# One load's source rows in another order: 64 pairs outermost instead of two runs of 64

## The chip, the cores and the metric

The kernel runs on one core of one Trainium2 chip. The metric is the device time of one execution in microseconds; lower is better. The time before is the median of three runs.

## The reference

Two independent spectral layers on 2048 rows of 512 numbers in float32, whose outputs are laid side by side.

```python
X = jnp.fft.rfft2(x, axes=(-2, -1)) * (w_r + 1j * w_i)     # A
y = jnp.fft.irfft2(X, s=(S, D), axes=(-2, -1))

a = jnp.einsum("bsd,ed->bse", x, dft_hid_re)               # B
b = jnp.einsum("bsd,ed->bse", x, dft_hid_im)
y = jnp.einsum("ts,bse->bte", dft_seq_re, a) - jnp.einsum("ts,bse->bte", dft_seq_im, b)
```

The four DFT matrices of B are inputs, 2048 x 2048 twice and 512 x 512 twice.

## The kernel before

Both transforms are done by matmuls with small tables that the program carries. B does not multiply by its big input matrices: it assumes that they are DFT matrices, transforms with its own tables, and compares every element of the inputs with them on the side (a flag tells at the end whether a slow path, which does multiply, has to run). So 34 blocks of 1 MB are loaded and compared.

The order of the work on PE, DVE, ACT and SP is written out by hand: each step registers itself under a name, and the string `PLAN` lists the names in the order in which they are issued. Each engine works off its own instructions in this order, and a step that waits holds all that stands behind it on its engine. Steps that matter here, with their lines:

- `xa`, `fold`, `hid`, `zs`, `f16_`, `ys` (L325 to L362): A's forward transform, in eight pieces. `hid7` and `f16_7` are the last piece's two groups of matmuls on PE, `zs7` is the copy on ACT (L351) between them, and `ys` (L362) writes the result to `fz`.
- Then eight slots n = 0 to 7, each with one residue of the frequencies: `w` loads its weights (L387) and its table `fi` (L391; L260 for slot 2, whose table is `fi0`), both on SP; `tr` transposes on PE (L404), `ez` copies on ACT (L408), `sf` combines on DVE (L414 to L416; `sx2` in slot 2, L437), `fwd` transforms on PE (L423; L427 in slot 2), `prod` and `comb` multiply with the weights on DVE (L454 to L466), `inv` transforms back on PE (L484, L487), `ev` copies on ACT (L491). In slot 2 the ACT step `spy` stands between `comb` and `inv`.
- B's x goes in 16 groups of 128 rows, four to a buffer: `xb0` to `xb15` load them (L581; the last group, L583 to L585, in three pieces), `xr0` to `xr3` copy the mirrored columns of a buffer on ACT (L594, L595), `al` multiplies a group with the table `fb` on PE (L605, L606), and `av` copies on ACT (L610).
- `cl` loads a block of B's matrices on SP (L712), `cc` compares it on DVE (L700). The tables of this comparison are `tt`. `late` is a table load from POOL.
- `bh`, `hv`, `ro`, `y1` to `y3`, `pt` finish B; `hi`, `eu`, `g16_`, `sc`, `eo`, `st` are A's inverse (L519 to L546).

On SP the loads stand in the order xb0 to xb3, cl5 to cl8, xb4 to xb7, w2 and fi0, xb8 to xb11, cl9 to cl12, w3, fi3, w4, fi4, cl13, w5, fi5, xb12 to xb15, cl14, cl15, w6, fi6, w7, fi7, cl16 and so on. The blocks of `cl`, `xa` and `xb` share six buffers of 1 MB, so a load waits for the last reader of its buffer. Besides, SP's loads take turns on eight semaphores: each waits until the load eight places ahead of it has landed.

A group g of `xb` holds the rows lo = 16 + 64 n onward and the rows low = 1984 - 64 n onward, 64 of each, for n < 15. The table `fb` has one row for each partition; a matmul with it sums over the 128 rows of a group, so which row lies on which partition is free as long as x and `fb` agree.

Of the kernel before, what the change touches and what calls it, by code (L numbers as in the profile page):

```python
# [15 lines left out]
S, D = 2048, 512  # L16
# [25 lines left out]
def _ang(n, period):  # L42
    return 2 * np.pi * (np.asarray(n, dtype=np.int64) % period) / period
# [34 lines left out]
def _b_rows():  # L78

    c = np.arange(128)  # L80
    return np.stack([np.where(c < 64, 16 * c, 8 + 16 * (c - 64))] + [e + 16 * c for e in range(1, 8)])


def _tables_b():

    order = [3, 5, 7, 9, 11, 13, 15, 1, 0, 2, 4, 6, 8, 10, 12, 14]
    a = np.arange(16)
    fb = np.zeros((2, 2, 4, 16, 8, 16))
    for kind in range(2):
        for at, k in enumerate(order):  # L90
            e = k // 2 if k > 1 else 8 * k

            def wave(shift, part):
                th = 2 * np.pi * (a + shift) * e / 16
                return -np.sin(th) if part else np.cos(th)

            top, low, sg = (k % 2, 1 - k % 2, 1 - 2 * (k % 2)) if k > 1 else (0, 0, 1)
            for n in range(4):
                if kind and n == 3:
                    fb[kind, 0, 3, :, 3, at] = wave(0.5 if k > 1 else 0, top)  # L100
                    fb[kind, 1, 0, :, 7, at] = wave(0, top)
                    continue
                fb[kind, 0, n, :, n, at] = wave(0, top)
                fb[kind, 1, 3 - n, :, n, at] = wave(1, top)
                fb[kind, 0, n, :, 4 + n, at] = sg * wave(0, low)
                fb[kind, 1, 3 - n, :, 4 + n, at] = -sg * wave(1, low)

    fb = fb.reshape(2, 128, 8, 16).transpose(0, 1, 3, 2)
    fbs = np.stack([np.concatenate([fb[:, :, 7:], v * fb], 2) for v in (1, -1)], 1)

    rows = _b_rows()
    p = (1 + 4 * np.arange(16)[:, None] + np.arange(4)).reshape(16, 4)
    mb = np.zeros((11, 16, 8, 128))
    for e in range(8):
        th = _ang(p[:, :, None] * rows[e], S)
        if e:
            mb[e - 1, :, :4], mb[e - 1, :, 4:] = np.cos(th), np.sin(th)
            mb[e - 1, 15, 3] = (-1.0) ** np.arange(128)
            mb[e - 1, 15, 7] = 1.0
        else:  # L120
            first = np.arange(128) < 64
            for i, m in enumerate((first, ~first)):
                mb[7 + i, :, :4] = np.cos(th) * m
                mb[9 + i, :, 4:] = -np.sin(th) * m
                mb[7 + i, 15, 7] = m
                mb[9 + i, 15, 7] = 0.0
                mb[9 + i, 15, 3] = -np.sin(th[15, 3]) * m
    alt = np.zeros((16, 8, 1))
    alt[:, :4, 0] = np.cos(np.pi * p)
    alt[15, 7] = 1.0  # L130
    mb = np.concatenate([mb.reshape(11, 128, 128).transpose(1, 0, 2).reshape(128, -1), alt.reshape(128, 1)], 1)
    hc = np.zeros((128, 2, 257))
    f = np.arange(257)
    hc[:, 0] = np.cos(_ang(np.outer(np.arange(128), f), D))
    hc[0, 0] = 1 - f % 2
    hc[0, 1] = f % 2
    turn = np.array([(S - rows[o]) % S if o else np.where(np.arange(128) == 0, 1024, (S - rows[0]) % S)
                     for o in range(8)]).T
    return fbs.transpose(2, 0, 1, 3, 4), mb, hc, turn


def _tables():
# [29 lines left out]
    ht = np.stack([np.cos(th), -np.sin(th)]).reshape(2, 2, 128, 257).transpose(2, 1, 0, 3)  # L172
    odd = np.array([1.0, -1.0]) * np.where(np.arange(128) % 2, -1.0, 1.0)[:, None]
    fb, mb, hc, turn = _tables_b()
    d = np.arange(256)
    hf = np.zeros((256, 2, 2, 128))
# [46 lines left out]
def kernel(  # L223
# [16 lines left out]
    mm, TT, load = pe.matmul, dve.tensor_tensor, sync.dma_start  # L240
# [10 lines left out]
    def step(name):  # L251
        def add(f):
            assert name not in steps
            steps[name] = f
        return add

    def const(name, *shape, src=None, by=None):
        t = sp.tile([P, *shape], F32, name=name)
        if src is not None:
            by.dma_start(t, src)  # L260
        return t
# [5 lines left out]
    def bank_b(name):  # L267
        at[name] = ps_b.tile([P, 512], F32, name="pb")
        return at[name]

    def block(name):
        at[name] = sp.tile([P, 2048], F32, name="blk", bufs=NB)
        return at[name]
# [280 lines left out]
    fb = const("fb", 2, 2, 200)  # L554
# [14 lines left out]
    def along(q):  # L569
        src = xb.rearrange("b a d -> (b a) d")  # L570

        def load_group(g):
            n = 4 * q + g

            @step(f"xb{n}")
            def _():
                if g == 0:
                    at["x", q] = block(("xb", q)).rearrange("p (g d) -> p g d", g=4)
                x, lo, low = at["x", q], 16 + 64 * n, 1984 - 64 * n
                if n < 15:  # L580
                    load(x[:, g], bass.AP(xb.tensor, lo * D, [[(low - lo) * D, 2], [D, 64], [1, D]]))  # L581
                else:
                    load(x[:64, g], src[lo : lo + 64])  # L583
                    load(x[64:80, g], src[:16])
                    load(x[80:, g], src[low + 16 : low + 64])  # L585

        for g in range(4):
            load_group(g)

        @step(f"xr{q}")  # L590
        def _():
            x = at["x", q]
            xr = at["xr", q] = sp.tile([P, 4, 256], F32, name="xr")
            act.copy(xr[:, :, 0], x[:, :, 256])  # L594
            act.copy(xr[:, :, 1:], x[:, :, 511:256:-1])  # L595

        def group(g):
            n = 4 * q + g

            @step(f"al{n}")  # L600
            def _():
                bank, x, xr = bank_b(("al", n)), at["x", q], at["xr", q]
                for c, (lo, w) in enumerate(((0, 200), (200, 144))):
                    k = slice(128 * c, 128 * c + 128)
                    mm(bank[:, lo : lo + w], x[:, g, k], fb[:, n // 15, 0, :w], start=True, stop=False)  # L605
                    mm(bank[:, lo : lo + w], xr[:, g, k], fb[:, n // 15, 1, :w], start=False, stop=True)  # L606

            @step(f"av{n}")
            def _():
                act.copy(yall[:, :, 8 * n : 8 * n + 8], at["al", n][:, :344].rearrange("p (s j) -> p s j", j=8))  # L610

        for g in range(4):
            group(g)
# [286 lines left out]
```

## Time and profile before

| what | value |
|---|---|
| median of three runs (lowest, highest) | 276.13 us (276.02, 276.51) |
| the profiled execution | 275.29 us, span 273.2 us |
| mean granted TensorE clock | 0.857 |
| busy: PE, DVE, ACT, POOL | 188.9, 156.3, 83.5, 22.5 us |
| moved by DMA | 66.24 MB, mean 242 GB/s |

Of the chain of work that ended last, 33% is put down to DMA, 32% to PE, 21% to SP's queue and 9% to DVE; the largest line in it is L581 on SP's queue with 14%.

Times are in microseconds from the start of the span. In the forty slices each digit is the busy share of 1/40 of the span, in tenths. In a table by stages, each engine's busy time is followed by the number of its instructions, then the granted PE clock, the mean busy share of the core's 16 DMA engines, and the rate. In a row of waits stand the engine and line that waited, what it waited for, the sum, the count and the longest. In a timeline row stand start and length, and in brackets the idle time before it and what ended that. SPq is SP issuing a DMA: the length is the time for which the issue held SP.

### The profile page before, as it was taken

To read this page: it belongs to the slowest core of one execution; us is meant where nothing else is said; L and a number is where in the kernel's file an instruction comes from. 1 tells how busy PE (TensorE), PEld (TensorE's weight loads), DVE (VectorE), ACT (ScalarE), POOL (GpSimd) and SP (SyncE) were. 2 spreads that over 40 slices of the span, in tenths; PEclk is the share of its full clock that TensorE was granted. 3 is DMA by queue.
4 is the path that set the end of the run, shared out by engine and by line. 5 is a ranking of instruction groups with operands and counts; after the bars stand their busy time and mean duration, and the time that the engine had idled before them with its cause. 6 is when DMAs were issued, how large, how long until landed. Compare 5 with 4: busy or idle time off the path is not lost.

```text
span 273.2 us, 2751 instructions
## 1 busy us (share of the span) xinstructions
PE 188.9 (69%) x1017; PEld 161.7 (59%) x1017; DVE 156.3 (57%) x217; ACT 83.5 (31%) x114; POOL 22.5 (8%) x32
## 2 busy tenths in 40 slices
PE   5699999500991019910089309999799999999930
PEld 1589999500980018910069309788378888999930
DVE  0730891001979501203937704999994599899970
ACT  1026465004740031503004014324335434543210
POOL 3000000000000000000000000001222245220110
PEclk9999999955797557975579957999979999999995
DMA  7999991298221611399911882690958999999913
GB/s 253 406 409 410 421 370 57 82 302 282 89 85 51 178 50 52 115 294 371 324 51 52 228 247 102 176 379 4 324 193 343 421 379 380 419 420 420 387 55 117
DMA packets 19393, 66.24 MB, mean 242 GB/s; under 512 B 1550, under 2 KB 2446, under 8 KB 18478
## 3 DMA queue, kind: packets, MB, share of 16 engines
q1 hardware_dynamic: 16574, 56.33, 57.2%
q0 software_dynamic: 2656, 9.08, 8.7%
q10 hardware_dynamic: 144, 0.59, 0.6%
q8 instruction: 10, 0.16, 0.2%
q14 instruction: 9, 0.07, 0.1%
HBM read 57.61 MB, written 8.39 MB: 242 GB/s over the span
## 4 chain that ended last, share of the span: by engine, by line
DMA 33%; PE 32%; SPq 21%; DVE 9%; ACT 2%; issue 1%; ACTq 0%; DVEq 0%
SPq L581 14%; PE pa L519 10%; DMA blk<-in_cm 8%; DMA fi<-tab_fi 8%; DMA w<-in_wa 7%; DMA blk<-in_xb 6%; PE pa L531 5%; SPq L712 4%; DMA blk<-in_xa 4%; PE pa L484 3%; DVE work L458 3%; DVE blk L700 2%; PE pa L427 2%; PE pb L631 2%; PE pb L643 2%; SPq L387 2%
## 5 line engine op out<-in xcount | busy, mean ns | idle before, releaser
L700 DVE SCALAR_TENSOR_TENSOR blk<-blk,odd,tt 128x2048 f32<-128x2048 f32 x16 | 37.1, 2349 | 39.9 <-DMA blk<-in_cm 39.8
L700 DVE SCALAR_TENSOR_TENSOR blk<-blk,tt 128x2048 f32<-128x2048 f32 (+2 forms) x24 | 41.4, 1755 | 2.6 <-ACT tt L740 2.2
L346 PE MATMUL pa<-ta,work 128*128 128x256 f32 x128 | 31.5, 404 | 3.5 <-DVE work L334 3.5
L346 PEld LDWEIGHTS pa<-ta,work 128*128 128x128 f32 x128 | 25.6, 204 | 8.2 <-DVE work L334 4.4
L519 PE MATMUL pa<-ta,fz 128*128 128x256 f32 x128 | 29.5, 386 | 0.0
L519 PEld LDWEIGHTS pa<-ta,fz 128*128 128x128 f32 x128 | 28.9, 305 | 0.4 <-issue 0.2
L358 PE MATMUL pa<-ta,work 128*128 128x128 f32 x128 | 17.3, 293 | 17.0 <-ACT work L351 17.0
L423 PE MATMUL pa<-work,fi 128*128 128x512 f32 x28 | 14.4, 652 | 20.1 <-DMA fi<-tab_fi 20.1
L358 PEld LDWEIGHTS pa<-ta,work 128*128 128x128 f32 x128 | 17.0, 209 | 17.5 <-ACT work L351 17.2
L606 PE MATMUL pb<-fb,xr 128*128 128x200 f32 (+1 forms) x64 | 15.8, 330 | 11.3 <-ACT xr L595 11.3
L458 DVE TENSOR_TENSOR work<-pa,w 128x1024 f32<-128x1024 f32 x14 | 16.5, 1219 | 8.7 <-ACT work L473 5.7
L423 PEld LDWEIGHTS pa<-work,fi 128*128 128x128 f32 x28 | 5.4, 209 | 25.2 <-DVE work L416 20.3
L594 ACT COPY xr<-blk 128x4 f32<-128x4 f32 x4 | 0.8, 198 | 60.4 <-DMA blk<-in_xb 47.5
L427 PE MATMUL pa<-work,fi 128*128 128x256 f32 x16 | 6.2, 570 | 18.0 <-DMA fi<-tab_fi 18.0
L606 PEld LDWEIGHTS pb<-fb,xr 128*128 128x128 f32 x64 | 11.5, 204 | 11.6 <-ACT xr L595 11.6
L362 ACT COPY fz<-pa 128x1024 f32<-128x1024 f32 x8 | 15.4, 1931 | 4.8 <-PE pa L358 4.8
L484 PE MATMUL pa<-fi,work 128*128 128x128 f32 x112 | 15.3, 295 | 2.1 <-DVE work L466 2.1
L427 PEld LDWEIGHTS pa<-work,fi 128*128 128x128 f32 x16 | 4.7, 304 | 19.9 <-ACT work L408 18.8
L484 PEld LDWEIGHTS pa<-fi,work 128*128 128x128 f32 x112 | 14.8, 211 | 2.6 <-DVE work L466 2.5
L605 PE MATMUL pb<-fb,blk 128*128 128x200 f32 (+1 forms) x64 | 15.4, 325 | 0.0
L531 PEld LDWEIGHTS pa<-ta,work 128*128 128x128 f32 x128 | 15.1, 192 | 0.2
L351 ACT COPY work<-pa 128x1024 f32<-128x1024 f32 x8 | 8.1, 1018 | 22.9 <-PE pa L346 22.9
(94 smaller groups left out, 265.8 us busy)
## 6 DMA issues: line engine op xcount, KB each, us to landing
blk<-in_cm SPq DMA_DIRECT2D x32, 1024.0 KB, 14.5
tt<-tab_tt SPq DMA_DIRECT2D x4, 1026.0 KB
w<-in_wa SPq DMA_DIRECT2D x8, 512.0 KB, 18.0
out_a<-work POOLq DMA_DIRECT2D x4, 1024.0 KB, 8.6
blk<-in_xb SPq DMA_DIRECT2D x15, 256.0 KB
blk<-in_xa SPq DMA_DIRECT2D x4, 512.0 KB
blk<-in_xa SPq DMA_DIRECT2D x2, 1024.0 KB
blk<-in_wd SPq DMA_DIRECT2D x2, 1024.0 KB
```

The lines of the kernel that those rows point to most:

```text
L346: mm(pd[:, r, h], us(b)[:, h, c, k, 128 * r : 128 * r + 128], hf[:, k, h], start=k == 0, stop=k == 1)
L358: mm(y[:, r, c], zs[:, r, 128 * c : 128 * c + 128], f16, start=True, stop=True)
L362: act.copy(fz.rearrange("p c k (n g) -> p g (c k n)", g=16)[:, i::8], flat(at["py", i]))
L423: mm(flat(px[:, h]), ft[:, 0], flat(t[:, h]), start=True, stop=True)
L427: mm(px[:, h, i], ft[:, 2 * i + j], z[:, j, h], start=j == 0, stop=j == 1)
L458: TT(out=m[:, h].rearrange("p i (r q) f -> p i r (q f)", r=2), in0=x2, in1=w2, op=MUL)
L484: mm(pi[:, i, q], lhs[i], it[:, 0], start=True, stop=True)
L519: mm(pu[:, k, h], gz[:, 2 * h + q, 2 * j + k], at["di"][:, h, q], start=q == 0, stop=q == 1)
L531: mm(po[:, k, q // 2, q % 2], u[:, k, q], at["g16"], start=True, stop=True)
L581: load(x[:, g], bass.AP(xb.tensor, lo * D, [[(low - lo) * D, 2], [D, 64], [1, D]]))
L606: mm(bank[:, lo : lo + w], xr[:, g, k], fb[:, n // 15, 1, :w], start=False, stop=True)
L700: dve.scalar_tensor_tensor(raw, raw, k, v, op0=MUL, op1=ALU.not_equal, accum_out=stat[:, i : i + 1])
```

## The change

The source of a group's load has its first two steps exchanged. Before, it walked two runs of 64 rows: partitions 0 to 63 held the low rows, 64 to 127 the high ones. Now it walks 64 pairs, each a low row and a high row: partition 2j holds row lo + j, partition 2j + 1 row low + j. The rows of the table `fb` for these groups are permuted in the same way on the host. The last group's three pieces and its table stay as they were. Every engine has the same instructions in the same order as before.

```diff
     fb = fb.reshape(2, 128, 8, 16).transpose(0, 1, 3, 2)
+    fb[0] = fb[0].reshape(2, 64, 16, 8).transpose(1, 0, 2, 3).reshape(128, 16, 8)
     fbs = np.stack([np.concatenate([fb[:, :, 7:], v * fb], 2) for v in (1, -1)], 1)
...
                 x, lo, low = at["x", q], 16 + 64 * n, 1984 - 64 * n
                 if n < 15:
-                    load(x[:, g], bass.AP(xb.tensor, lo * D, [[(low - lo) * D, 2], [D, 64], [1, D]]))
+                    load(x[:, g], bass.AP(xb.tensor, lo * D, [[D, 64], [(low - lo) * D, 2], [1, D]]))
                 else:
```

## The prediction

> **What bounds the kernel now.** I read the page's forty slices first, then busy time and DMA by stage, then the waits of PE and ACT, then the timelines of PE and DVE at the places where PE stops.
>
> ```profile
> DMA  7999991298221611399911882690958999999913
> GB/s 253 406 409 410 421 370 57 82 302 282 89 85 51 178 50 52 115 294 371 324 51 52 228 247 102 176 379 4 324 193 343 421 379 380 419 420 420 387 55 117
> ```
>
> The DMA engines are not idle in the middle of the span, and they are not full either: again and again the rate stands at 50 GB/s. The stages, with the last two columns as the mean busy share of the 16 DMA engines and what they moved:
>
> ```profile
> core 0: us, PE busy (x) PEld busy (x) DVE busy (x) ACT busy (x) POOL busy (x), PEclk, DMA share, GB/s
> 30.00:40.00 10.00, 10.00 (x62) 9.17 (x61) 10.00 (x10) 5.50 (x5) 0.00 (x0) 1.00 1.03 412
> 42.00:52.00 10.00, 9.88 (x62) 8.94 (x60) 0.00 (x0) 2.59 (x2) 0.00 (x0) 1.00 0.14 52
> 54.00:64.00 10.00, 0.00 (x0) 0.00 (x0) 0.00 (x0) 0.00 (x0) 0.00 (x0) 0.56 1.02 298
> 94.00:114.00 20.00, 12.78 (x68) 11.61 (x69) 2.89 (x6) 5.62 (x10) 0.00 (x0) 0.69 0.14 52
> 137.00:151.00 14.00, 13.49 (x75) 10.72 (x76) 7.36 (x12) 3.95 (x9) 0.00 (x0) 0.88 0.13 52
> 219.00:262.00 43.00, 42.91 (x242) 40.06 (x241) 40.63 (x46) 17.03 (x24) 11.03 (x11) 1.00 0.95 379
> ```
>
> A share of 0.13 to 0.14 is 2 of 16 engines, and 52 GB/s is 2 x 26, while 16 busy engines move 412 (2 x 26 is an eighth of it). So in these stretches exactly two engines work. What they carry is seen on SP, which issues the loads (least, median, longest issue):
>
> ```profile
> L712 SPq DMA_DIRECT2D blk<-in_cm x32: 367/368/5063, 4.2 to 246.2; - x32
> L581 SPq DMA_DIRECT2D blk<-in_xb x15: 543/5062/11112, 31.7 to 140.1; - x15
> L585 SPq DMA_DIRECT2D blk<-in_xb x1: 413/413/413, 151.0 to 151.0; - x1
> ```
>
> The fifteen group loads of B's x hold SP for 5.06 us each, and 256 KB in 5.06 us is 51.8 GB/s: each is drained by two engines, and SP stands behind them. An issue that isn't held takes 0.54 us, so the 5 us are not the making of the load. Everything that SP issues later, cm blocks, w and fi, starts late. Those who wait:
>
> ```profile
> ACT xr L594 <- DMA blk<-in_xb: 47.5, 3, 19.1
> DVE blk L700 <- DMA blk<-in_cm: 40.2, 4, 25.5
> PE pa L423 <- DMA fi<-tab_fi: 20.1, 1, 20.1
> PE pa L427 <- DMA fi<-tab_fi: 18.0, 1, 18.0
> PE pa L358 <- ACT work L351: 17.0, 1, 17.0
> PE pb L606 <- ACT xr L595: 11.3, 1, 11.3
> ```
>
> The four PE waits, 66.4 us together, have one root. xr0 and xr3 wait for x itself; the copy ahead of f16_7 stands behind xr0 on ACT; fi of fwd2 and fwd3 are queued on SP behind eight of the slow loads.
>
> **The change, part by part.** No instruction moves, is added or is removed on any engine. *The table* is permuted on the host: nothing. *The load* has the same 128 rows of 2 KB, with 64 instead of 2 as the outermost count of its source. Its price is bounded by two rows: the cm loads, with 128 partitions outermost, run on all engines (412 GB/s: 0.64 us for 256 KB), and the old load on two (5.06 us). 64 pairs are nearer to the first, so I take 16 engines, 0.64 us, and keep 5.06 for the range.
>
> The Trainium skill (DMA: Bandwidth & Descriptors, section "Why a DMA increments its semaphore by 16 and not by 1") states that the engine count is the largest number up to 16 that divides the slowest dimension of both access patterns; that is 2 for 2 against 128 partitions, and 16 for 64 against 128. The trace agrees with the 2 (share 0.14); no run here shows the other yet.
>
> Fifteen loads shrink from 75.9 to 9.6 us of queue. What that is worth is worked out along the path. Names: al, av, cc, fwd, prod and so on are steps of the plan, with the slot or group behind.
>
> *From 40 us to fwd0.* The backlog ahead of the first x load is drained at about 40.6 in either kernel (before, the rate falls there, a mean of 135 GB/s in this stretch):
>
> ```profile
> 40.00:42.00 2.00, 2.00 (x17) 1.92 (x16) 1.86 (x2) 2.00 (x3) 0.00 (x0) 1.00 0.37 135
> ```
>
> ```profile
> 46.48 3.62 PE L346 MATMUL pa<-ta,work 128*128 128x256 f32 x16
> 49.94 1.95 PE L358 MATMUL pa<-ta,work 128*128 128x128 f32 x16
> 68.86 3.63 PE L358 MATMUL pa<-ta,work 128*128 128x128 f32 x16 [16.98 <-ACT work L351]
> 79.62 3.60 PE L423 MATMUL pa<-work,fi 128*128 128x512 f32 x8
> ```
>
> Four x loads, 1.05 MB at 412, then end at 43.2. For the lag from last byte to landing the nearest row is a small lone store:
>
> ```profile
> out_b<-yb POOLq DMA_DIRECT2D x2, 128.0 KB, 4.0
> ```
>
> That bounds it by 0 and 3.7 (4.0 less 0.3 at 412); I take 2. x lands at 45.2. ACT then has three steps in its order, from these rows:
>
> ```profile
> 65.14 1.03 ACT L595 COPY xr<-blk 128x1020 f32<-128x1020 f32 x1
> L362 ACT COPY fz<-pa 128x1024 f32<-128x1024 f32 x8 | 15.4, 1931 | 4.8 <-PE pa L358 4.8
> L351 ACT COPY work<-pa 128x1024 f32<-128x1024 f32 x8 | 8.1, 1018 | 22.9 <-PE pa L346 22.9
> ```
>
> xr0 (1.1 with its small copy), ys5 (1.9) and zs7 (1.0); zs7 also needs hid7, done at 46.48 + 3.62 = 50.1. So zs7 is done at 51.1, ahead of f16_6's end at 51.9, and f16_7 follows at once, at full clock: 1.95 instead of 3.63 us. It ends at 53.8. From f16_7's end (72.5) to fwd0 (79.62) PE had 7.1 us of work without a wait: fwd0 starts at 61.0, if its input is there. That hangs on cc8 and sf0 on DVE, so on cl8: x, four cm blocks and the late table, 5.8 MB from 40.6, end at 54.8 and land at 56.8.
>
> ```profile
> L700 DVE SCALAR_TENSOR_TENSOR blk<-blk,tt 128x2048 f32<-128x2048 f32 x16 | 36.4, 2288 | 0.4 <-DMA blk<-in_cm 0.4
> L414 DVE TENSOR_TENSOR work<-pa,work 128x512 f32<-128x512 f32 x7 | 4.8, 686 | 13.8 <-ACT work L408 8.6 <-PE pa L484 5.2
> L415 DVE TENSOR_TENSOR work<-work,pa 128x512 f32<-128x512 f32 x7 | 4.8, 680 | 0.3
> ```
>
> cc8 (2.3) and sf0 (1.4) end at 60.5. It fits by half a microsecond.
>
> *From prod0 to prod5.* Here DVE is next in line:
>
> ```profile
> 81.53 2.35 DVE L458 TENSOR_TENSOR work<-pa,w 128x1024 f32<-128x1024 f32 x2 [1.44 <-PE pa L423]
> 175.89 2.36 DVE L458 TENSOR_TENSOR work<-pa,w 128x1024 f32<-128x1024 f32 x2 [0.43 <-PE pa L423]
> 198.32 0.17 DVE L466 TENSOR_TENSOR work<-work,sgn 128x4 f32<-128x4 f32 x1
> 198.54 3.64 PE L484 MATMUL pa<-fi,work 128*128 128x128 f32 x16 [2.11 <-DVE work L466]
> 258.18 3.73 PE L531 MATMUL pa<-ta,work 128*128 128x128 f32 x32
> ```
>
> ```profile
> 81.50:176.00 94.50, 42.47 (x64) 0.73 0.51 162
> 176.00:198.50 22.50, 21.95 (x33) 1.00 0.66 241
> ```
>
> Before, prod0 starts at 81.53, now at 61.0 + 1.9 = 62.9. From there to prod5 DVE has 42.5 us of work in 94.4. Without waits it needs 42.5 x 22.5 / 21.95 = 43.5, as in the next stretch, where it had none to speak of. prod5 starts at 106.4 instead of 175.9, **69.5 us earlier**.
>
> What must be there on time for that: fi of fwd3. All that is loaded from 40.6 up to it (12 x loads, 8 cm blocks, late, w2, fi0, w3, fi3) is 13.8 MB: at 412 it ends at 74.1, landed 76.1. When PE comes to fwd3 is told by the end of fwd2 and of tr4 before:
>
> ```profile
> 107.27 1.04 PE L404 MATMUL pa<-eye,fz 128*128 128x128 f32 x8
> 116.38 1.04 PE L404 MATMUL pa<-eye,fz 128*128 128x128 f32 x8
> ```
>
> fwd0 and fwd1 take 3.6, fwd2 3.6 at full clock (16 matmuls of 256 columns, as in hid7), then 10.2 to tr4's end: 61.0 + 17.4 = 78.4. x for al12: its loads stand on SP behind w5, which waits for prod2 (82 us by the same counting); 1.7 MB more, landed at 88, wanted at 93. Both are hidden, the first with 2 us to spare.
>
> *From prod5 to the end* nothing changes: DVE carries the path to inv7 at 198.5, PE from there to 262 without a gap at clock 1.00, and in 219:262 the DMA engines are as full as before, since the cm blocks follow the compares that free their buffers.
>
> **The sum.** 18.6 up to prod0 and 50.9 up to prod5 make 69.5. Span 273.2 to 203.7; the profiled execution 275.29 to 205.8; the median of the runs stands 0.84 above that execution, so 276.13 to **206.6 us**. DVE takes over as the bound in the middle; were PE alone the bound, its four waits and the half-clock work after them (some 7 us) would give 202 to 203.
>
> The Trainium skill (DMA: Bandwidth & Descriptors, section "Where 436 GB/s comes from") speaks against the full gain: loads from HBM are bound at about 358 GB/s. By it, fi3 would land at 81.1, 3 us late, and cl8 would come 2 us late as well, and the time would be some 209. The measured 412 differs, and decides.
>
> **The rivals.**
>
> *A new DMA wait.* All 16 engines are busy in 54:64 as well, and yet move only 298. I put that down to the x loads still on two of them, since the rate is low just while they are. If instead such traffic runs at 298 by itself, cl8 lands at 62.2, fwd0 comes 5 us later, and fi3 lands near 89 instead of the 83 then wanted; with 1 to 2 us of slack on DVE that is 9 to 10 us: 216.
>
> *No change.* If the engine count hangs on something else than the outermost count, the loads stay on two engines, and the time is 276. Against it: every load with many rows outermost fills the engines.
>
> *Slower.* If a pair can't be matched with two partitions and each load falls to one engine, it takes 10.1 us, and the fifteen add 75.9 us in the same places where removing 66 gives 69: about 350. It decides as soon as fewer than two engines work on them. Against it: the cm loads, too, have a source of three steps, and are spread.
>
> **How the numbers follow.** The forecast gets 0.77, the new wait 0.15, no change 0.05, slower 0.03. The range runs from PE's own bound, 203, to the new wait, 216, and leaves out the two cases without a gain. Faster by over 0.2% (about what a measurement of this kernel can tell from no change) 0.92, within 0.2% 0.05, slower 0.03.
>
> **What the new profile would show.** The x loads issue in 0.4 to 0.6 us, and no stretch stands at a share of 0.13 and 52 GB/s. The four PE waits are gone, and so is ACT's wait for x. From prod0 to prod5 DVE is idle for 1 or 2 us. PE's busy time falls by about 7 us, since work after a pause ran at half clock. From inv7 to the end it takes the same 75 us. I am wrong in the path if PE still waits for fi, or DVE for cm, for more than a few microseconds; wrong in the root if x loads still hold SP.

## The result and the profile after

The change takes the median from 276.18 to **205.65 us** (four runs of each; 204.06 to 206.28 after), a ratio of 0.744 with a 95% interval of 0.739 to 0.748. The forecast was 206.6 us. The profiled execution took 205.54 us, its span is 203.4 us (forecast 203.7), and the mean granted clock rose from 0.857 to 0.961. Where one run of a kernel lies over 1.5% above its fastest, as one of `short_cc9_12` below does, the ratio leaves it out.

Busy times, the two DMA rows of the forty slices and the packet count, from the page of the kernel after:

```profile
PE 182.2 (90%) x1017; PEld 156.5 (77%) x1017; DVE 155.6 (76%) x217; ACT 83.6 (41%) x114; POOL 23.0 (11%) x32
...
DMA  6999999999999996779599029398999999999241
GB/s 197 396 417 412 427 376 421 401 413 406 398 413 405 407 388 233 255 270 358 148 337 338 29 58 356 153 338 310 428 352 395 367 416 421 421 419 414 114 174 47
DMA packets 19603, 66.24 MB, mean 326 GB/s; under 512 B 1760, under 2 KB 2656, under 8 KB 18688
```

The same bytes move, and up to 76 us the rate now stands near 400. The two low slices left in the middle (29 and 58, from 112 to 122 us) are of another kind: the busy share is under 0.3 there, and SP waits for buffers that DVE's compares free, as SP's waits show (the longest, 14.7 us, falls there):

```profile
SPq L713 <- DVE blk L701: 60.0, 14, 14.7
```

The packet count is the plainest sign of what changed. The page before has this line:

```profile
DMA packets 19393, 66.24 MB, mean 242 GB/s; under 512 B 1550, under 2 KB 2446, under 8 KB 18478
```

The difference is 210, all of it in packets under 512 B. Each engine that takes part in a load closes it with one small packet, so fifteen loads that went from 2 engines to 16 leave 15 x 14 = 210 more. The x loads on SP after (least, median and longest issue), and by stages a stretch with x loads among the others and the one that DVE was to bound:

```profile
L582 SPq DMA_DIRECT2D blk<-in_xb x15: 534/547/2002, 31.5 to 83.2; - x15
```

```profile
core 0: us, PE busy (x) PEld busy (x) DVE busy (x) ACT busy (x) POOL busy (x), PEclk, DMA share, GB/s
42.00:76.00 34.00, 34.00 (x222) 30.71 (x221) 24.95 (x35) 19.87 (x27) 0.54 (x1) 1.00 1.03 406
62.40:105.80 43.40, 41.64 (x268) 35.70 (x267) 41.77 (x64) 18.05 (x34) 0.00 (x0) 1.00 0.85 308
```

The issue fell from 5.06 to 0.55 us, PE works through 42 to 76 us without a pause at clock 1.00. From prod0 to prod5 DVE and PE are busy almost alike, 41.77 and 41.64 of 43.40 us; which of them is the bound, this row alone does not tell, an experiment below does. All waits of PE by what it waited for, and DVE's steps on which the forecast's path rests (cc8, prod0, prod5):

```profile
PE pb L778 <- DVE rs L776: 4.5, 1, 4.5
PE pa L485 <- DVE work L467: 3.8, 1, 3.8
PE pa L347 <- DVE work L335: 3.7, 1, 3.7
PE pa L305 <- DVE zero L279: 1.3, 1, 1.3
PE pa L488 <- ACT work L475: 1.0, 1, 1.0
PE pa L485 <- DVE work L459: 0.8, 1, 0.8
PE pa L485 <- DVE w L455: 0.3, 1, 0.3
```

```profile
55.69 2.29 DVE L701 SCALAR_TENSOR_TENSOR blk<-blk,tt 128x2048 f32<-128x2048 f32 x1 [0.30 <-DMA blk<-in_cm]
...
62.47 2.35 DVE L459 TENSOR_TENSOR work<-pa,w 128x1024 f32<-128x1024 f32 x2 [1.62 <-PE pa L424]
...
105.74 2.36 DVE L459 TENSOR_TENSOR work<-pa,w 128x1024 f32<-128x1024 f32 x2
```

No wait of PE for fi, for x or for ACT behind x is left, and ACT's own wait for x fell from 47.5 to 1.0 us. What is left on PE is at the start (3.7 and 1.3), at the very end (4.5), before inv7 (3.8), where PE waits for DVE, and three short waits in the middle, 2.1 us together.

### The profile page after: what moved, and what is told of

It is laid out like the page before. It is cut to its first block, busy times and chain, and to the rows that moved or that the text cites. A ratio compares the mean times of both kernels' runs of the same rounds, so it can differ in the third digit from the quotient of the medians.

```text
span 203.4 us, 2751 instructions
## 1 busy us (share of the span) xinstructions
PE 182.2 (90%) x1017; PEld 156.5 (77%) x1017; DVE 155.6 (76%) x217; ACT 83.6 (41%) x114; POOL 23.0 (11%) x32
## 4 chain that ended last, share of the span: by engine, by line
PE 58%; DVE 34%; DMA 3%; issue 2%; POOL 0%; ACT 0%; DVEq 0%; ACTq 0%; POOLq 0%
PE pa L347 15%; PE pa L520 14%; DVE work L459 9%; DVE blk L701 8%; PE pa L532 7%; PE pa L359 7%; DMA wsp_sb<-in_wsp 3%; PE pb L644 3%; DVE work L463 3%; DVE work L465 3%; PE pb L632 3%; DVE work L466 2%; DVE work L464 2%; PE pa L485 2%; DVE work L415 2%
## 5 line engine op out<-in xcount | busy, mean ns | idle before, releaser
L347 PEld LDWEIGHTS pa<-ta,work 128*128 128x128 f32 x128 | 25.4, 203 | 8.1 <-DVE work L335 4.6
L520 PE MATMUL pa<-ta,fz 128*128 128x256 f32 x128 | 29.5, 386 | 0.0
L520 PEld LDWEIGHTS pa<-ta,fz 128*128 128x128 f32 x128 | 28.9, 305 | 0.4 <-issue 0.2
L485 PE MATMUL pa<-fi,work 128*128 128x128 f32 x112 | 15.8, 300 | 4.8 <-DVE work L467 3.8
L352 ACT COPY work<-pa 128x1024 f32<-128x1024 f32 x8 | 8.1, 1012 | 24.1 <-PE pa L347 24.1
L363 ACT COPY fz<-pa 128x1024 f32<-128x1024 f32 x8 | 15.3, 1942 | 3.6 <-PE pa L359 3.6
L338 DVE TENSOR_TENSOR work<-blk 128x1024 f32<-128x1024 f32 x6 | 7.1, 1221 | 12.7 <-PE pa L347 12.7
L525 ACT COPY work<-pa 128x1024 f32<-128x1024 f32 x8 | 8.1, 1013 | 20.8 <-PE pa L520 20.8
L359 PEld LDWEIGHTS pa<-ta,work 128*128 128x128 f32 x128 | 15.4, 192 | 0.4
L359 PE MATMUL pa<-ta,work 128*128 128x128 f32 x128 | 15.4, 275 | 0.0
L532 PEld LDWEIGHTS pa<-ta,work 128*128 128x128 f32 x128 | 15.1, 192 | 0.2
L532 PE MATMUL pa<-ta,work 128*128 128x128 f32 x128 | 15.1, 275 | 0.0
L541 DVE TENSOR_TENSOR work<-pa,work 128x512 f32<-128x512 f32 x16 | 10.3, 684 | 6.2 <-ACT work L536 6.2
L606 PE MATMUL pb<-fb,blk 128*128 128x200 f32 (+1 forms) x64 | 14.6, 309 | 0.0
L607 PE MATMUL pb<-fb,xr 128*128 128x200 f32 (+1 forms) x64 | 14.6, 309 | 0.0
L492 ACT COPY fz<-pa 128x1024 f32<-128x1024 f32 x8 | 8.1, 1011 | 12.6 <-PE pa L485 9.5
L424 PE MATMUL pa<-work,fi 128*128 128x512 f32 x28 | 12.8, 592 | 0.0
```

The lines of the kernel that those rows point to most:

```text
L347: mm(pd[:, r, h], us(b)[:, h, c, k, 128 * r : 128 * r + 128], hf[:, k, h], start=k == 0, stop=k == 1)
L359: mm(y[:, r, c], zs[:, r, 128 * c : 128 * c + 128], f16, start=True, stop=True)
L363: act.copy(fz.rearrange("p c k (n g) -> p g (c k n)", g=16)[:, i::8], flat(at["py", i]))
L424: mm(flat(px[:, h]), ft[:, 0], flat(t[:, h]), start=True, stop=True)
L485: mm(pi[:, i, q], lhs[i], it[:, 0], start=True, stop=True)
L520: mm(pu[:, k, h], gz[:, 2 * h + q, 2 * j + k], at["di"][:, h, q], start=q == 0, stop=q == 1)
```

## The experiments

Single runs stand beside a run of the kernel before on the same chip, which took 276.4 to 276.6 us each time.

### Is it the interleaving, or the outermost count?

The change does two things at once: neighbouring partitions now hold a low and a high row, and the source's outermost count goes from 2 to 64. `halves` drops the first: two loads of 64 plain rows for each group, in the row layout and with the table of before.

```diff
-load(x[:, g], bass.AP(xb.tensor, lo * D, [[(low - lo) * D, 2], [D, 64], [1, D]]))
+load(x[:64, g], src[lo : lo + 64])
+load(x[64:, g], src[low : low + 64])
```

> The kernel before with each group's load cut into two loads of 64 rows (low run, high run): rows and table lie as before, nothing is interleaved. If the outermost count (64) sets the number of engines: 16 engines, 205 to 208 us, no stretch at 52 GB/s, and DMA packets 19393 + 30 x 16 - 15 x 2 = 19843, if each engine that takes part adds one small completion packet to a load. If interleaving low and high rows is what made the loads fast (rows near each other in memory for neighbouring partitions), the stretches at 52 GB/s stay and the time is near 276.

Measured: 213.48 us. Without any interleaving 63 of 71 us are gained. The packet count agrees with 30 loads on 16 engines each (19393 less 30 plus 480 is 19843):

```profile
DMA packets 19844, 66.25 MB, mean 313 GB/s; under 512 B 2000, under 2 KB 2896, under 8 KB 18928
```

But the time is 5.5 to 8.5 us above what was expected, and the timelines give a reason. SP's issue of the first cm blocks behind the x loads, in `halves` and then after:

```profile
44.28 4.21 SPq L713 DMA_DIRECT2D blk<-in_cm  x4
```

```profile
40.35 2.42 SPq L713 DMA_DIRECT2D blk<-in_cm  x4
```

And two of DVE's waits for those blocks in `halves` (cc5 and cc8), then PE's wait for the step behind them (fwd0), each from its engine's timeline:

```profile
51.95 2.35 DVE L701 SCALAR_TENSOR_TENSOR blk<-blk,odd,tt 128x2048 f32<-128x2048 f32 x1 [10.13 <-DMA blk<-in_cm]
...
63.15 2.29 DVE L701 SCALAR_TENSOR_TENSOR blk<-blk,tt 128x2048 f32<-128x2048 f32 x1 [3.78 <-DMA blk<-in_cm]
```

```profile
66.99 6.28 PE L423 MATMUL pa<-work,fi 128*128 128x512 f32 x8 [6.03 <-DVE work L416]
```

Each of SP's loads waits until the load eight places ahead has landed. The timelines after show it: w2, fi0 and xb8 stand eight places behind cl5, cl6 and cl7; they are issued at 47.44, 50.45 and 53.06, just as those blocks land (cc5, cc6 and cc7, which wait for them, start at 47.53, 50.54 and 53.10). Twice as many x loads of half the size take twice the places, so cm blocks are issued 3.9 us later. From 40 to 48 us `halves` moves 236 to 239 GB/s, after the change it is 408 to 413; cc8 starts at 63.15 instead of 55.69, PE stands 6.0 us ahead of fwd0, and the matmuls behind that wait take 6.28 instead of 3.60 us. This was read from the traces of two kernels; the turns of eight themselves were not varied, so that they are the cause is not shown.

### The same rows in steps, with 2, 4, 8 and 16 outermost

`halves_o2` to `halves_o16` take the same two loads, but let the source walk K runs of rows with a stride, so that its outermost count is K; the table's rows follow. The bytes, the loads and the row length are the same in all four, and the rows are interleaved over the partitions in all of them. The diff against the change, with K = 4:

```diff
-    fb[0] = fb[0].reshape(2, 64, 16, 8).transpose(1, 0, 2, 3).reshape(128, 16, 8)
+    fb[0] = fb[0].reshape(2, 16, 4, 16, 8).transpose(0, 2, 1, 3, 4).reshape(128, 16, 8)
...
-load(x[:, g], bass.AP(xb.tensor, lo * D, [[D, 64], [(low - lo) * D, 2], [1, D]]))
+load(x[:64, g], bass.AP(xb.tensor, lo * D, [[D, 4], [4 * D, 16], [1, D]]))
+load(x[64:, g], bass.AP(xb.tensor, low * D, [[D, 4], [4 * D, 16], [1, D]]))
```

> The same with 2 as the outermost count: even rows of a run, then its odd rows. If the count sets the engines: two again, stretches at a share of 0.13 and 52 GB/s, 19393 + 30 x 2 - 30 = 19423 packets, and the time of the kernel before or a little more, 274 to 286. If it was long runs of neighbouring rows on one engine that made the load slow, this one, whose rows are as interleaved as with 4 or 8, should stay below 234.

> The same with 4 as the outermost count. If the count sets the engines: 4, stretches at a share of 0.25 and some 104 GB/s, packets 19393 + 30 x 4 - 30 = 19483. Up to fi of fwd3 four engines carry 10.7 MB / 16 + 3.15 MB / 4 = 1.46 MB, 57 us, and fi lands at 99 instead of 76, 20 us late: about 228 us (220 to 238). If it falls to two engines: 276; if the count doesn't matter: 206.

> As the two loads of 64 rows, but each with 8 as the outermost count of its source (rows taken in steps of 8; the table rows follow). If the count sets the engines: 8 of them, stretches at a share of 0.5 and some 206 GB/s, packets 19393 + 30 x 8 - 30 = 19603. These 8 carry all of x and their part of the rest: up to fi of fwd3 each has 10.7 MB / 16 + 3.15 MB / 8 = 1.06 MB, 41 us at 25.8 GB/s instead of 34, so fi lands some 5 us later than it is wanted: about 209 us. If 8 is enough for all 16 engines: 206. If every source with a small outermost count falls to two engines: 276.

> Two loads of 64 rows for each group, with 16 as the outermost count (rows in steps of 16; the table rows follow). If the engines are the outermost count up to 16, this is no other than 64: 213.5 us as with the plain halves, 19843 packets. If more rows outermost are worth more: a time between those of 8 (216.2) and 64, and fewer packets.

Measured, with a stretch of each in which x loads run alone (share and rate are the last two columns of its row; with 16 no x loads run alone for long, so its stretch has cm blocks among them):

| outermost | time, us | share | GB/s | packets above before |
|---|---|---|---|---|
| 2 | 277.32 | 0.13 | 50 | 31 |
| 4 | 234.03 | 0.26 | 99 | 91 |
| 8 | 216.20 | 0.53 | 203 | 211 |
| 16 | 210.06 | 1.01 | 411 | 451 |

The rows for 2, 4, 8 and 16, each from its own kernel:

```profile
78.00:88.00 10.00, 7.31 (x39) 5.04 (x36) 8.08 (x15) 2.34 (x5) 0.00 (x0) 1.00 0.13 50
```

```profile
78.00:84.00 6.00, 1.30 (x3) 1.16 (x4) 5.43 (x9) 2.05 (x3) 0.00 (x0) 0.53 0.26 99
```

```profile
66.00:70.00 4.00, 0.46 (x2) 0.09 (x1) 3.83 (x6) 2.05 (x3) 0.00 (x0) 0.88 0.53 203
```

```profile
46.00:52.00 6.00, 6.00 (x41) 5.59 (x41) 1.83 (x1) 4.18 (x5) 0.00 (x0) 1.00 1.01 411
```

Share and rate double with the count, and the packets count the engines (30 x K in place of before's 30, within one). So the engines that carry a load are as many as its outermost count, from 2 to 16, and with 64 the packets count 16 again. `halves_o2` has its rows interleaved and is as slow as before; so interleaving as such is worth nothing. The Trainium skill (DMA: Bandwidth & Descriptors, section "Why a DMA increments its semaphore by 16 and not by 1") has the rule, the largest number up to 16 that divides the slowest dimension of both access patterns; the four counts agree with it. They are all powers of two, so a rule that merely takes the count, up to 16, would agree as well: no count here tells the two apart.

The time does not fall in proportion, since waits go one by one as their loads become early enough. PE's waits for fi in `halves_o4`, where half the load time is left:

```profile
PE pa L428 <- DMA fi<-tab_fi: 7.8, 1, 7.8
```

Before, this wait was 18.0. The times for 2 and 4 are within what was expected. For 8, "about 209" was 7 us too low: PE waits 6.1 us for fi, near the 5 us by which it was expected late, but the 16 matmuls of fwd2 behind the first of these waits then take 6.60 instead of 3.62 us, and the thirty loads cost something of their own, as the 210.06 us of 16 show. `halves_o16` and `halves` are nearly the same work and differ by 3.4 us in single runs on two chips; that difference is not explained.

### Is it SP's queue that is held, or x that is late?

Two things followed from two slow engines: SP was held for 5.06 us at each load, and x landed late. `pool_runs` is before with only this: the fifteen loads, two runs outermost as they were, are issued by POOL.

```diff
-load(x[:, g], bass.AP(xb.tensor, lo * D, [[(low - lo) * D, 2], [D, 64], [1, D]]))
+pool.dma_start(x[:, g], bass.AP(xb.tensor, lo * D, [[(low - lo) * D, 2], [D, 64], [1, D]]))
```

> The kernel before with its fifteen loads (two runs of 64 rows outermost, rows and table as before) issued by POOL instead of SP. SP is then never held by x, so w, fi and cm come as early as in the changed kernel. If it was the held queue that cost most, and x itself, drained by two engines one load after the other from about 31 us, is late by less: PE's waits for fi (20.1 and 18.0 us) go, a part of ACT's wait for x stays, and the time is some 220 us (212 to 232). If the lateness of x itself carried the cost: 260 to 276. If POOL's loads run on more engines than SP's: 206 to 210, and the packets tell by how many.

Measured: 234.12 us, 2 us above the range that was expected. PE's waits for ACT in `pool_runs`, its x loads (size, median us from issue to landing), POOL's queue and the packet count of its page, and a stretch of it by stages:

```profile
PE pa L358 <- ACT work L351: 17.5, 1, 17.5
PE pb L606 <- ACT xr L595: 7.3, 1, 7.3
...
PE pa L427 <- ACT work L408: 2.5, 1, 2.5
```

```profile
blk<-in_xb POOLq DMA_DIRECT2D x15, 256.0 KB, 24.5
```

```profile
DMA packets 25364, 66.30 MB, mean 285 GB/s; under 512 B 8480, under 2 KB 9376, under 8 KB 24448
...
q0 software_dynamic: 10576, 13.07, 19.3%
```

```profile
40.00:66.00 26.00, 10.72 (x67) 9.71 (x65) 9.32 (x8) 5.00 (x6) 6.32 (x8) 0.75 1.07 267
```

After, the same 256 KB land 7.9 us after their issue:

```profile
blk<-in_xb SPq DMA_DIRECT2D x15, 256.0 KB, 7.9
```

The two waits for fi (20.1 and 18.0) are gone; the two behind x itself (17.0 and 11.3) are 17.5 and 7.3. So with SP free 42 us come back, and by the waits that are left the last 28 come from x that is late. The split is not shown apart from the change of queue: POOL's loads don't look like SP's. Against before there are 25364 - 19393 = 5971 packets more, 398 for each load, where SP left 130 (128 rows and 2 to close it). Those under 512 B rose by 8480 - 1550 = 6930, so the larger ones fell by about 960, 64 for each load: its data goes in 64 packets instead of 128, and with them come some 464 small ones. And in 40:66 all engines are busy at only 267 GB/s. Part of the 28 us may come from that; how many engines carry one of POOL's loads was not told apart.

### Does DVE bound the stretch from prod0 to prod5?

`short_cc9_12` is the change with four of the compares there (cc9 to cc12) cut from 2048 columns to 64. It leaves out the comparison of most of those four blocks. `after_again` is the change itself, beside it on the same chip.

```diff
+c = slice(0, 16) if 9 <= i <= 12 else slice(0, 512)
-unequal(..., four(raw), t[...], ...)
+unequal(..., four(raw)[:, :, c], (t[...])[:, :, c], ...)
```

> The changed kernel unaltered, as the base for the runs beside it: 204 to 207 us.

> The changed kernel with four compares (cc9 to cc12, all between prod0 and prod5) cut to 64 of their 2048 columns, so most of these four blocks is not compared; loads and order as before. DVE has some 8.8 us less work in the stretch in which I hold it to be the bound. If DVE is the bound there and PE comes next: PE's waits for DVE (1.0, 0.8, 0.3 and 3.8 us) go, the time falls by 4 to 6 us, to 200 to 201, and not by 8.8. If PE was the bound already: no change. If DVE alone sets the end: 8.8 us less, 197.

Measured: `after_again` 206.17 us (204.29 to 206.58, ratio 0.747, interval 0.745 to 0.749), `short_cc9_12` 198.66 us (197.91 to 202.29, ratio 0.718, interval 0.715 to 0.721): 7.5 us less, more than expected. In `short_cc9_12`, two stretches by stages, from near prod0 on and behind inv7, and inv7's matmuls in PE's timeline:

```profile
62.30:101.00 38.70, 38.70 (x257) 34.20 (x256) 33.43 (x63) 18.04 (x34) 0.00 (x0) 1.00 0.90 323
128.00:135.00 7.00, 7.00 (x30) 5.88 (x31) 4.94 (x16) 3.31 (x7) 1.71 (x2) 1.00 0.87 314
```

```profile
123.72 2.05 PE L485 MATMUL pa<-fi,work 128*128 128x128 f32 x16 [2.11 <-DVE work L467]
```

The stretch behind inv7 and its matmuls after:

```profile
128.00:135.00 7.00, 6.61 (x25) 5.34 (x26) 6.37 (x16) 2.22 (x3) 1.78 (x2) 0.64 0.51 165
```

```profile
128.39 3.79 PE L485 MATMUL pa<-fi,work 128*128 128x128 f32 x16 [3.77 <-DVE work L467]
```

PE now runs without a pause where it was busy for 41.64 of 43.40 us, and with less work on DVE alone the stretch from prod0 to prod5 shrinks from 43.27 to 38.78 us, so DVE was the bound there; PE is next. inv7 starts 4.67 us earlier. The rest is the clock: after, inv7's group takes 3.79 us and the stretch is granted 0.64; in `short_cc9_12` it takes 2.05 at 1.00. From inv7's start to the end the one needs 203.4 - 128.39 = 75.0 us, the other 196.5 - 123.72 = 72.8. All of the difference arises at once: PE comes to its next L520 group 7.31 us behind inv7's start after, and 5.10 us in `short_cc9_12`. So a wait of 3.8 us on PE cost 2.2 us more after it was over; in the trace of `after_again`, where the wait is the same 3.77 us, that group comes 6.75 us behind, and the cost is 1.7.

### Can the compares be moved behind that wait?

DVE does cc13 to cc15 in the stretch before inv7 that it bounds, and has room after it. `cc14_behind` moves cc14, and the load cl20 that follows it, behind inv7 in the plan; `cc13_14_behind` moves cc13 and cl19 as well.

```diff
-... ev6 cc14 cl18 cl19 rx ro1 ry prod7 y11 cl20 bh2 pt0 comb7 hv2 y21 inv7 cc15
+... ev6 cl18 cl19 rx ro1 ry prod7 y11 bh2 pt0 comb7 hv2 y21 inv7 cc14 cl20 cc15
```

> The changed kernel with one compare (cc14) moved from ahead of prod7 to behind comb7 and y21, and the load that takes its buffer (cl20) behind it. inv7 on PE waits 3.8 us for comb7; comb7 comes 2.3 us earlier. If DVE bounds this stretch and PE all that follows: 2.3 us faster, 203.3. If the later buffer pushes the loads of the last stretch, which already fill the DMA engines, or DVE falls behind later: no change.

> The same with two compares (cc13 and cc14) and their two loads. comb7 comes 4.5 us earlier, PE's wait of 3.8 us goes: 3.8 us faster, 201.9, if nothing behind them is late. If the two loads, 2 MB or 5 us of DMA, slip into the stretch in which the DMA engines are full up to the end: up to 5 us is given back, and the time is 203 to 207.

Measured: `cc14_behind` 203.57 us (201.77 to 204.26, ratio 0.736, interval 0.731 to 0.740), `cc13_14_behind` 204.16 us (203.29 to 204.54, ratio 0.738, interval 0.736 to 0.741). The median of the first is 2.6 us (1.3%) below that of `after_again`, the intervals don't touch, and its highest time, 204.26, lies just below the lowest of `after_again`, 204.29. Its waits of PE at inv7 and later:

```profile
125.22 3.56 PE L485 MATMUL pa<-fi,work 128*128 128x128 f32 x16 [1.49 <-DVE work L467]
...
182.71 3.89 PE L520 MATMUL pa<-ta,fz 128*128 128x256 f32 x16 [1.16 <-ACT work L525]
```

In `cc13_14_behind`, inv7 in PE's timeline, then prod7 ahead of it and a compare far behind it in DVE's:

```profile
126.09 3.27 PE L485 MATMUL pa<-fi,work 128*128 128x128 f32 x16 [1.38 <-DVE work L467]
```

```profile
120.82 2.36 DVE L459 TENSOR_TENSOR work<-pa,w 128x1024 f32<-128x1024 f32 x2 [2.27 <-PE pa L424]
...
174.67 2.35 DVE L701 SCALAR_TENSOR_TENSOR blk<-blk,odd,tt 128x2048 f32<-128x2048 f32 x1 [0.85 <-DMA blk<-in_cm]
```

Moving one compare shortens PE's wait at inv7 from 3.77 to 1.49 us and loses part of it later: from inv7's start to the end it takes 76.2 us, against 75.0 after, with a new wait of 1.16 us for ACT in it. Moving two gains nothing more at inv7, because the room that it makes on DVE is filled by another wait: prod7 now waits 2.27 us for PE's fwd7, which it did not with one compare moved. Counted from prod5, inv7 starts 20.38 us later with one compare moved and 20.27 with two, against 22.65 after. The loads behind it, which follow the compares that free their buffers, do come later, and DVE waits for them, but that costs no time here: from inv7 to the end it takes 76.0 us with two moved. So, by these traces, it is PE and not the late loads that stops the second move, other than was expected. The profiled executions differ by less than the medians (204.29 us in `after_again`, 203.59 in `cc14_behind`), so the traces do not account for the whole 2.6 us.

## Why the prediction was right, point by point

- **The root.** Two engines for each x load, and SP held by them: shown by the four counts (2, 4, 8, 16), by the 210 packets and by the issue time. The rule on the number of engines that the prediction cited had been seen only for 2; it holds for 64 against 128 too. The price taken for the load, that of a load on all 16 engines, is what the trace shows.
- **From 40 us to fwd0.** x0 to x3 were to land at 45.2, and ACT copies the first of them at 45.6 (least, median and longest copy, then the first and the last start):

```profile
L595 ACT COPY xr<-blk x4: 192/200/202, 45.6 to 91.1; 128x4 f32<-128x4 f32 x4
```

  cc8 was to start at 56.8 and starts at 55.69; prod0 was to start at 62.9 and starts at 62.47. Its block thus landed 1.1 us ahead of the estimate, which had two parts, 412 GB/s from 40.6 us on and 2 us from the last byte to landing; which was too long is not told apart. cc8 still waited 0.30 us for it, so DMA sets the start of cc8. It does not set prod0, which waits 1.62 us for PE (its row stands with the result). fwd0 starts at 60.55 (forecast 61.0) right behind PE's own work, and its input from sf0 is done at 59.40. So PE sets this place, as forecast, with 1.1 us to spare on DVE instead of half a microsecond.
- **From prod0 to prod5.** 43.27 us against 43.5, with DVE idle for 1.6 of 43.4, as forecast (1 to 2). fi3 and x were on time: there is no PE wait for either. `short_cc9_12` shows by experiment that DVE is the bound here.
- **From prod5 to the end.** 75.0 us from inv7 against 74.7 before, and from prod5 to inv7 22.65 us in both.
- **The term that was mis-sized: PE's own bound,** "202 to 203", the lower end of the range. With DVE's load taken away the median is 198.66. The step took "some 7 us" for work at half clock after waits. PE's busy time fell by 188.9 - 182.2 = 6.7 after, as forecast for the change, but to 179.3 in `short_cc9_12`:

```profile
PE 179.3 (91%) x1017; PEld 154.6 (79%) x1017; DVE 147.3 (75%) x217; ACT 83.5 (43%) x114; POOL 22.5 (11%) x32
```

  That is 9.6 us less than before; 66.4 + 9.6 = 76.0 against 273.2 - 196.5 = 76.7 in span. The bound left out that inv7 ran at half clock before as well, behind its wait of 2.11 us; without the drop it takes 2.05 instead of 3.64 us. The forecast itself did not hang on it, since DVE sets the end.
- **The new DMA wait** did not come: 406 GB/s in 42:76 with x loads among the others. That x on two engines was what held 54:64 at 298 GB/s is not confirmed, though. Rates like that with busy engines are seen where no x load is in flight, before and after:

```profile
174.00:176.00 2.00, 2.00 (x7) 0.93 (x6) 1.57 (x4) 1.01 (x1) 0.00 (x0) 1.00 0.95 295
```

```profile
102.00:110.00 8.00, 8.00 (x33) 5.04 (x32) 7.83 (x10) 2.05 (x3) 0.00 (x0) 1.00 0.96 325
```

  So the forecast was right on this rival in part by luck: it was dismissed for a reason that the row of 174:176 before already weakens. What lowers the rate there stays open.
- **No change, and slower:** both are ruled out by the issue time, 0.55 us where two engines took 5.06 and one would have taken 10.1.
- **The 358 GB/s** that the prediction cited from the Trainium skill, and by which the time would have been some 209, do not bind here: 406 over 34 us.

## What to carry to other kernels

Where the busy share of the DMA engines stands at n/16 and the rate at n times 26 GB/s, look at the outermost count of the load's source: put a dimension there that is a multiple of 16, in the DRAM access pattern as well as over the partitions, and let a table or the host absorb the new row order. A load on few engines costs twice, in its own landing and in the queue that it holds, and the second is read from its issue time. Cutting it into more loads instead was 4 to 8 us slower here, by the traces for the places that it takes among those in flight. Before promising the sum of the waits, work out which engine is next, and what a pause leaves behind on the clock.

## What the runs showed of the hardware that was not expected

- **Pauses and the clock.** A wait of 2.11 us before inv7 left the clock at 1.00 in `short_cc9_12` (the group took 2.05 us), and the same 2.11 us before the change was followed by a group of 3.64 us. One of 1.49 us in `cc14_behind` was followed by 3.56. So the length of a pause of this size does not tell whether the clock halves. The Trainium skill (TensorE: Matmul & The Clock Gate, Part 1) says that the clock follows an activity window that runs free, so that the point of a change depends on where in the window the matmuls fall; the runs can be read that way, but none varied the phase alone. In its section "Why this matters for your kernels" it asks for no gaps over about 3 us; here a gap of 1.49 us was already followed by half clock, and the measurement decides.
- **POOL's loads have other packets than SP's:** for the same load, 64 large packets and some 464 small ones, where SP left 128 and 2.
- **All 16 engines busy is not yet full rate:** 267 GB/s over 26 us in `pool_runs` at a share of 1.07, against 406 at 1.03 after. A share alone doesn't show it; the rate beside it does.
